# Rebuilding float32 weights from float64 words: an exponent, a product and a float addition replaced by one integer addition

## The chip, the core and the metric

The kernel runs as one program on one core of a Trainium2 chip. The metric is the device time of one execution in microseconds, the median of several executions. Five engines work side by side, each on its own in-order list of instructions: TensorE (PE, matrix products), VectorE (DVE), ScalarE (ACT), GpSimd (POOL) and SyncE (SP, which here only issues transfers). They meet through semaphores.

## The reference

A causal attention with a compressive memory feeds two gated feed-forward layers (B=4, H=8, S=576, D=64; 2304 tokens of 512 channels):

```python
local = softmax(causal(q @ k.T / 8)) @ v
mem   = (phi(q) @ M_prev) / (phi(q) @ z_prev + 1e-6)      # phi(x) = elu(x) + 1
x     = sigmoid(beta) * mem + (1 - sigmoid(beta)) * local
x     = (sigmoid(x @ w_gate) * (x @ w_val)) @ w_out       # width 1536
h     = x @ w_in                                          # width 2048
out   = (h * clip(h + 3, 0, 6) / 6) @ w_out2
```

The five weight matrices of the two layers come to the device as float64. [...]

## The kernel before

**Phase A** runs 32 attention visits (a pair of heads and a range of rows each) and, interleaved with them on PE, six of the twelve hidden blocks of the first layer for the first 1872 tokens. In a visit PE makes scores (`score_part`), DVE takes the row maximum from them (L324), ACT the exponentials (L362), ACT or DVE the normalisation (L390, L392), PE transposes (L402), ACT copies the transposed blocks to SBUF (L404), and PE multiplies with the values (`pv`, L426). POOL makes the products for the memory norm (`prep_phi`, L301 and L305) and writes the memory columns into the rows that are transposed (`memory_rows`, L377). `moe_a` is the interleaved first layer; its gated product on DVE is L488.

**Phase B** does the rest of the first layer: per hidden block the gate and value products (L233 to L235 into tile `g`), a tanh on ACT, the gated product on DVE (L674), its split (L228 on ACT, L229 on DVE, tile `hs`), and the second product into `acc`.

**Phase C** does the second layer by sums of blocks with seven products in place of eight. For each of three groups of tokens `c_load` reads the activations into `xh`, `c_sums` makes three sums on POOL (L735), and `c_block` splits each of seven operands into a tile `xq` (L228, L229; the operand `t4` has one more sum on POOL, L754). The products are L787, those of the second matrix L822. Tile `xt` of the sums and one half of `xh` use the two buffers `wst` in which the float64 weights are staged, so the first group's sums start only when the last weight has been converted.

**Weights** are staged by `w_load` (two matrices' blocks at a time, two buffers `wst`) and converted by `value`: ACT takes the absolute value of the high word (L151), DVE clamps it (L152), cuts and shifts the bits (L153), puts sign and top exponent bit back (L154, in place in the high word), cuts out the exponent (L155), scales the low word by it (L157) and adds it (L158). `convert` and `convert_pair` then split the result into a rounded part (ACT, L163 or L201) and a remainder (DVE, L164 or L202). The work tile `wf` has one buffer. A call handles 1024 elements per partition in phase A (9 calls, "wide") and 512 later (50 calls, "narrow"; 4 of them stand late in phase A, 46 in phase B). The converted weights of phase C go to DRAM and are fetched back in phase C.

The order on PE is written out by hand in phases A and C. On the other engines, and on PE in phase B, a scheduler sets the order when the program is built, by costs of its own; each engine then keeps that order whatever the real durations are.

Of the kernel before, what the change touches and what calls it, by code (L numbers as in the profile page):

```python
# [8 lines left out]
F32 = mybir.dt.float32  # L9
F32R = mybir.dt.float32r  # L10
I32 = mybir.dt.int32
U32 = mybir.dt.uint32
AF = mybir.ActivationFunctionType
ALU = mybir.AluOpType
# [64 lines left out]
class Kernel:  # L79
# [64 lines left out]

    def value(self, st):

        nc = self.nc
        lo, hi = st[:, :, :, 0], st[:, :, :, 1]
        w = self.stage.tile([128, self.wide, 512], F32, name="wf", tag="wf", bufs=1)
        wi, hif, lof = w.bitcast(I32), hi.bitcast(F32), lo.bitcast(F32)  # L150
        nc.scalar.activation(w, hif, AF.Abs)  # L151
        nc.vector.tensor_scalar(w, w, HI_MIN, HI_MAX, op0=ALU.max, op1=ALU.min)  # L152
        nc.vector.tensor_scalar(wi, wi, 0x07FFFFFF, 3, op0=ALU.bitwise_and, op1=ALU.logical_shift_left)  # L153
        nc.vector.scalar_tensor_tensor(hi, hi, -0x40000000, wi, op0=ALU.bitwise_and, op1=ALU.bitwise_or)  # L154
        nc.vector.tensor_scalar(wi, hi, -0x800000, None, op0=ALU.bitwise_and)  # L155
        yield hif
        nc.vector.scalar_tensor_tensor(lof, lo.bitcast(U32), 2.0**-52, w, op0=ALU.mult, op1=ALU.mult)  # L157
        nc.vector.tensor_tensor(hif, hif, lof, op=ALU.add)  # L158

    def convert(self, sl, st):  # L160
        nc = self.nc
        for hif in self.value(st):
            nc.scalar.copy(sl[:, 0], hif)  # L163
        nc.vector.tensor_tensor(sl[:, 1], hif, sl[:, 0].bitcast(F32), op=ALU.subtract)  # L164

    def convert_pair(self, j, up, st):
# [807 lines left out]
```

## Time and profile before

| | |
|---|---|
| median of 3 runs | 1081.23 us (1079.56 to 1082.05) |
| the profiled execution | 1079.94 us, span 1078.2 us |
| busy, share of the span: PE / DVE / ACT / POOL | 96% / 63% / 51% / 8% |
| mean granted TensorE clock | 0.987 |

The span is the time from the first to the last instruction of that execution; what lies around it makes up the rest of its time. Phase A lasts from 0 to about 400 us, phase B to 684 us, phase C to the end. PE counts as busy while a matmul is in flight, so its share says when it had nothing to do, and not how fast it went. PE is waited for or waits; a wait of another engine costs time only if PE comes to wait for it.

### The profile page before, as it was taken

The page shows a single profiled execution, that of the slowest core. Times are in us where ns is not written, and L with a number is a line of the kernel's source. Part 1 is how long each engine was busy: PE and PEld are TensorE (multiplying, and loading weights), DVE is VectorE, ACT ScalarE, POOL GpSimd, SP SyncE. Part 2 cuts the span into 40 slices and gives each one's busy share as a digit, 9 for nine tenths or more (in the row PEclk, how much of TensorE's full clock was granted, in tenths as well). Part 3 has the DMA queues.
Part 4 walks back from the last instruction along what each step waited for, and adds up shares of the span by engine and source line. Part 5 has one row for each costly group of instructions (what it writes and reads, how often), then busy time and mean ns, then how long its engine had stood idle before and what let it go on. Part 6 is the DMA issues. An engine that isn't in the chain of part 4 may idle for free.

```text
span 1078.2 us, 16086 instructions
## 1 busy us (share of the span) xinstructions
PE 1037.6 (96%) x5824; PEld 890.3 (83%) x5824; DVE 684.2 (63%) x1602; ACT 551.5 (51%) x1191; POOL 83.2 (8%) x102
## 2 busy tenths in 40 slices
PE   4789999999999999999999999799999999999998
PEld 2457768877887899999888888688888888888886
DVE  7999885454455348899898988854355333643432
ACT  5989885576556644435434433434344333543432
POOL 3212211110111000000000000320002000000000
PEclk9879999999999999999999999899999999999999
DMA  6645642424242225227586776645305543044511
GB/s 217 220 170 182 202 129 68 141 79 120 59 134 79 64 85 175 93 102 260 216 292 221 257 250 221 228 178 215 122 27 184 186 148 135 1 153 190 215 40 59
DMA packets 66239, 164.87 MB, mean 153 GB/s; under 512 B 8432, under 2 KB 41712, under 8 KB 60272
## 3 DMA queue, kind: packets, MB, share of 16 engines
q1 hardware_dynamic: 66160, 163.85, 44.5%
q8 instruction: 46, 0.75, 0.3%
q14 instruction: 33, 0.27, 0.1%
HBM read 122.76 MB, written 41.06 MB: 152 GB/s over the span
## 4 chain that ended last, share of the span: by engine, by line
PE 85%; DVE 7%; ACT 3%; DMA 2%; issue 1%; POOL 1%; SPq 0%; POOLq 0%; ACTq 0%
PE acc L822 18%; PE pa L787 9%; PE pb L787 7%; PE g L235 6%; PE g L233 6%; PE g L234 6%; PE m L233 5%; PE m L234 5%; PE m L235 5%; PE pv L426 4%; PE t L402 4%; PE s L344 3%; PE acc L233 3%; PE acc L235 3%; PE acc L234 3%; DMA aux<-in_aux 2%
## 5 line engine op out<-in xcount | busy, mean ns | idle before, releaser
L822 PE MATMUL acc<-wslot,hs 128*128 128x512 f32 x864 | 227.8, 395 | 2.2 <-ACT hs L228 2.2
L822 PEld LDWEIGHTS acc<-wslot,hs 128*128 128x128 f32 x864 | 159.5, 188 | 27.7 <-ACT hs L228 3.5
L787 PE MATMUL pa<-xq,wslot 128*128 128x384 f32 x576 | 119.3, 342 | 7.3 <-ACT xq L228 5.4
L787 PEld LDWEIGHTS pa<-xq,wslot 128*128 128x128 f32 x576 | 105.1, 190 | 16.6 <-ACT xq L228 5.8
L235 PE MATMUL g<-xs,wslot 128*128 128x468 f32 (+1 forms) x288 | 106.1, 369 | 0.0
L234 PE MATMUL g<-xs,wslot 128*128 128x468 f32 (+1 forms) x288 | 105.6, 369 | 0.0
L233 PE MATMUL g<-xs,wslot 128*128 128x468 f32 (+1 forms) x288 | 103.9, 369 | 0.0
L362 ACT ACTIVATE P<-P,m 128x192 f32<-128x192 f32 (+4 forms) x144 | 84.1, 586 | 31.2 <-DVE m L324 29.8
L233 PE MATMUL m<-xs,wslot 128*128 128x312 f32 x288 | 93.7, 325 | 0.0
L787 PE MATMUL pb<-xq,wslot 128*128 128x384 f32 x432 | 89.1, 341 | 0.2 <-DVE xq L229 0.2
L234 PE MATMUL m<-xs,wslot 128*128 128x312 f32 x288 | 88.1, 306 | 0.0
L235 PE MATMUL m<-xs,wslot 128*128 128x312 f32 x288 | 87.8, 305 | 0.0
L344 PE MATMUL s<-qk 64*128 64x320 f32 (+3 forms) x320 | 70.8, 502 | 14.3 <-DMA qk<-in_qk 11.8
L787 PEld LDWEIGHTS pb<-xq,wslot 128*128 128x128 f32 x432 | 78.6, 189 | 7.0 <-DVE xq L229 0.7
L851 DVE TENSOR_TENSOR c<-pb,u 128x384 f32<-128x384 f32 x48 | 26.6, 555 | 88.1 <-ACT u L887 87.1
L402 PEld LDWEIGHTS t<-ident,P 128*128 128x128 f32 x464 | 53.8, 145 | 27.2 <-issue 14.5
L799 ACT ACTIVATE r<-c,three 128x384 f32<-128x384 f32 x72 | 44.2, 614 | 61.9 <-DVE c L851 61.9
L402 PE MATMUL t<-ident,P 128*128 128x128 f32 x464 | 68.4, 285 | 7.5 <-POOL P L377 4.1
L229 DVE TENSOR_TENSOR hs<-r,hs 128x384 fp32r<-128x384 f32 x96 | 55.9, 586 | 26.3 <-ACT hs L228 24.8
L404 ACT COPY T<-t 128x512 f32<-128x512 f32 (+2 forms) x128 | 65.7, 540 | 12.1 <-PE t L402 11.9
L324 DVE CUSTOM_DVE_ANT_0 P<-s,mask 128x320 f32<-128x320 f32 (+3 forms) x144 | 62.5, 451 | 14.5 <-PE s L344 14.2
L426 PE MATMUL pv<-T,aux 128*64 128x256 f32 (+2 forms) x512 | 63.4, 377 | 4.5 <-ACT T L404 4.5
(102 smaller groups left out, 1966.9 us busy)
## 6 DMA issues: line engine op xcount, KB each, us to landing
wst<-in_wm SPq DMA_DIRECT2D x68, 512.0 KB, 5.7
wslot<-wd SPq DMA_DIRECT2D x30, 1024.0 KB, 5.0
wd<-wslot SPq DMA_DIRECT2D x16, 1024.0 KB, 4.4
wslot<-wd SPq DMA_DIRECT2D x15, 768.0 KB, 6.3
wd<-wslot SPq DMA_DIRECT2D x8, 768.0 KB, 5.8
qk<-in_qk SPq DMA_DIRECT2D x32, 160.0 KB, 2.3
aux<-in_aux SPq DMA_DIRECT2D x16, 320.0 KB, 3.3
qk<-in_qk SPq DMA_DIRECT2D x16, 288.0 KB, 3.0
```

What stands on the lines that cost most here:

```text
L229: elo.tensor_tensor(lo, src, hi.bitcast(F32), op=ALU.subtract)
L233: nc.tensor.matmul(out, w[0], x[0], start=first, stop=False)
L234: nc.tensor.matmul(out, w[0], x[1], start=False, stop=False)
L235: nc.tensor.matmul(out, w[1], x[0], start=False, stop=last)
L324: self.nc.vector.tensor_tensor_reduce(out=self.row(v, rg, r, 64 + a, 64 + e), in0=ps, in1=mask, scale=-0.125, scalar=3.0e38 if a == 0 else ...
L344: nc.tensor.matmul(ps[:, : e - a], qk[rows, 0, q0 : q0 + 128], qk[rows, 1, a:e], start=True, stop=True)
L362: self.nc.scalar.activation(x, x, AF.Exp, bias=vs["m", rg][:, r : r + 1], scale=-1.0, accum_out=vs["l", rg][:, r : r + 1])
L402: nc.tensor.transpose(ps[:, 128 * n : 128 * n + 128], self.row(v, rg, r, 128 * j, 128 * j + 128), self.ident)
L404: nc.scalar.copy(pr["T", rg][:, 512 * k : 512 * k + c], ps[:, :c])
L426: nc.tensor.matmul(ps[rows, o : o + w], pr["v"][:, j, rows], T[:, c : c + w], start=(n == 0), stop=(n == last), skip_group_check=True,)
L787: nc.tensor.matmul(ps[:, :HC], w[:, i, b, cc], x[:, l, k], start=first and k == 0 and n == 0, stop=last and k == 1 and n == 2, skip_group_ ...
L822: nc.tensor.matmul(a, h[:, i, cc], w[:, l, f], start=first and f == 0 and n == 0, stop=last and f == 1 and n == 2)
```

## The change

The low word is scaled by 2^-29 and rounded to an integer, in place, on POOL (L155 of the new kernel). Sign and top exponent bit are put back into `wf` in place of the high word (L156, was L154). The sum of the two as 32-bit integers is the float32's bit pattern, with the carry into the exponent (L158). The rounded part is now copied from `wf` (L163). L155 and L157 of the old kernel, DVE instructions both, are gone. Line numbers of `value` move: old L151 to L153 are new L152 to L154.

```diff
     def value(self, st):
...
         lo, hi = st[:, :, :, 0], st[:, :, :, 1]
         w = self.stage.tile([128, self.wide, 512], F32, name="wf", tag="wf", bufs=1)
-        wi, hif, lof = w.bitcast(I32), hi.bitcast(F32), lo.bitcast(F32)
+        wi, hif = w.bitcast(I32), hi.bitcast(F32)
         nc.scalar.activation(w, hif, AF.Abs)
         nc.vector.tensor_scalar(w, w, HI_MIN, HI_MAX, op0=ALU.max, op1=ALU.min)
         nc.vector.tensor_scalar(wi, wi, 0x07FFFFFF, 3, op0=ALU.bitwise_and, op1=ALU.logical_shift_left)
-        nc.vector.scalar_tensor_tensor(hi, hi, -0x40000000, wi, op0=ALU.bitwise_and, op1=ALU.bitwise_or)
-        nc.vector.tensor_scalar(wi, hi, -0x800000, None, op0=ALU.bitwise_and)
-        yield hif
-        nc.vector.scalar_tensor_tensor(lof, lo.bitcast(U32), 2.0**-52, w, op0=ALU.mult, op1=ALU.mult)
-        nc.vector.tensor_tensor(hif, hif, lof, op=ALU.add)
+        nc.gpsimd.tensor_scalar(lo, lo.bitcast(U32), 2.0**-29, None, op0=ALU.mult)
+        nc.vector.scalar_tensor_tensor(wi, hi, -0x40000000, wi, op0=ALU.bitwise_and, op1=ALU.bitwise_or)
+        yield w, hif
+        nc.vector.tensor_tensor(hi, wi, lo, op=ALU.add)

     def convert(self, sl, st):
         nc = self.nc
-        for hif in self.value(st):
-            nc.scalar.copy(sl[:, 0], hif)
+        for w, hif in self.value(st):
+            nc.scalar.copy(sl[:, 0], w)
         nc.vector.tensor_tensor(sl[:, 1], hif, sl[:, 0].bitcast(F32), op=ALU.subtract)
```

On DVE at the end of phase B (L674 is the gated product of one hidden block, `xq` an operand of phase C, `c` the first result of phase C), the order before has the last remainder of a weight (L164) behind the last L674:

```order
L674 SCALAR_TENSOR_TENSOR th<-th,g 128x468
L152 TENSOR_SCALAR wf<-wf 128x512
L164 TENSOR_TENSOR wslot<-wst,wslot 128x512
L153 TENSOR_SCALAR wf<-wf 128x512
L229 TENSOR_TENSOR hs<-th,hs 128x468
L154 SCALAR_TENSOR_TENSOR wst<-wst,wf 128x512
L155 TENSOR_SCALAR wf<-wst 128x512
L157 SCALAR_TENSOR_TENSOR wst<-wst,wf 128x512
L158 TENSOR_TENSOR wst<-wst 128x512
L694 SCALAR_TENSOR_TENSOR xp<-acc,xp 128x468 x2
L164 TENSOR_TENSOR wslot<-wst,wslot 128x512
L694 SCALAR_TENSOR_TENSOR xp<-acc,xp 128x468 x2
```

The same engine with the change, from the last conversion on:

```order
L156 SCALAR_TENSOR_TENSOR wf<-wst,wf 128x512
L158 ISA wst<-wst,wf 128x512x2
L164 TENSOR_TENSOR wslot<-wst,wslot 128x512
L674 SCALAR_TENSOR_TENSOR th<-th,g 128x468
L694 SCALAR_TENSOR_TENSOR xp<-acc,xp 128x468 x2
L229 TENSOR_TENSOR hs<-th,hs 128x468
L694 SCALAR_TENSOR_TENSOR xp<-acc,xp 128x468 x2
L674 SCALAR_TENSOR_TENSOR th<-th,g 128x468
L229 TENSOR_TENSOR xq<-xh,xq 128x768 x2
L229 TENSOR_TENSOR hs<-th,hs 128x468
L674 SCALAR_TENSOR_TENSOR th<-th,g 128x468
L229 TENSOR_TENSOR xq<-xt,xq 128x768
```

The last conversion now stands ahead of the last six L674 (three of them are shown), and the operands `xq` of phase C stand among them. The addition is a custom instruction (ISA) over pairs of 16-bit halves, 512x2.

On DVE in phase A, around the first split of activations for the first layer (`xs` from `xc`), the order before has the second conversion's addition:

```order
L385 SCALAR_TENSOR_TENSOR l<-l,a_108 128x5
L306 TENSOR_REDUCE nr<-phw 128x5
L229 TENSOR_TENSOR xs_636<-xc,xs_636 128x312
L324 ISA P,m<-s,mask 128x320
L324 ISA m 128x1
L158 TENSOR_TENSOR wst<-wst 128x1024
```

With the change the third conversion's addition stands there:

```order
L154 TENSOR_SCALAR wf<-wf 128x1024
L229 TENSOR_TENSOR xs_632<-xc,xs_632 128x312
L156 SCALAR_TENSOR_TENSOR wf<-wst,wf 128x1024
L306 TENSOR_REDUCE nr<-phw 128x5
L324 ISA P,m<-s,mask 128x320
L324 ISA m 128x1
L158 ISA wst<-wst,wf 128x1024x2
```

Conversions have moved ahead of the attention: up to the first L488, 5 additions stood on DVE before and 7 stand there now, and on ACT 7 pairs of absolute value and copy in place of 5 ahead of the tanh that belongs to that L488.

On POOL at the start of phase A, the scaling joins the list between the products of a visit (L301, L305) and its memory columns (L377), where before L377 followed L305 at once:

```order
L301 TENSOR_TENSOR phw<-ph,zz 128x64
L305 TENSOR_TENSOR phw<-ph,zz 128x256
L155 TENSOR_SCALAR wst<-wst 128x1024
L377 TENSOR_TENSOR P<-ph,nr 128x5x64
L301 TENSOR_TENSOR phw<-ph,zz 128x64
L305 TENSOR_TENSOR phw<-ph,zz 128x256
L155 TENSOR_SCALAR wst<-wst 128x1024
```

Nine wide scalings stand in phase A; of the 50 narrow ones the last 46 follow each other ahead of the first L735. The order on PE is the same in phases A and C; in phase B some matmuls near the borders of token groups change places.

## Rows read from the trace of the kernel before

**Rows 1.** The page: span, and PE's busy time, share and instructions.

```profile
span 1078.2 us, 16086 instructions
...
PE 1037.6 (96%) x5824; PEld 890.3 (83%) x5824; DVE 684.2 (63%) x1602; ACT 551.5 (51%) x1191; POOL 83.2 (8%) x102
```

**Rows 2.** Busy us by stretch; columns PE, PEld, DVE, ACT, POOL, clock, DMA share, GB/s.

```profile
16.00:66.00 50.00, 37.81 (x200) 21.49 (x200) 49.26 (x136) 46.30 (x112) 11.64 (x14) 0.83 0.57 180
400.00:684.00 284.00, 283.89 (x1401) 258.33 (x1400) 254.56 (x477) 120.92 (x206) 0.00 (x0) 1.00 0.60 211
684.67:692.94 8.27, 2.33 (x6) 1.93 (x7) 7.03 (x6) 3.92 (x6) 8.19 (x4) 0.62 0.58 222
```

**Rows 3.** PE's timeline where phase C begins: start us, us, instruction, idle before it.

```profile
679.09 1.20 PE L787 MATMUL pa<-xq,wslot 128*128 128x384 f32 x6
...
683.51 0.38 PE L235 MATMUL acc<-hs,wslot 128*128 128x468 f32 x1
689.27 0.69 PE L787 MATMUL pa<-xq,wslot 128*128 128x384 f32 x1 [5.38 <-ACT xq L228]
691.30 1.97 PE L787 MATMUL pa<-xq,wslot 128*128 128x384 f32 x5 [1.34 <-DVE xq L229]
...
701.25 1.09 PE L822 MATMUL acc<-wslot,hs 128*128 128x512 f32 x4
```

**Rows 4.** POOL's timeline from 400 to 702 us, the first of its four rows.

```profile
684.67 1.81 POOL L735 TENSOR_TENSOR xt<-xh 128x768 f32<-128x768 f32 x1 [319.82 <-DVE wslot L164]
```

**Rows 5.** DVE's timeline from 640 to 702 us.

```profile
653.80 0.64 DVE L674 SCALAR_TENSOR_TENSOR th<-th,g 128x468 f32<-128x468 f32 x1 [0.59 <-PE g L235]
...
661.45 0.64 DVE L674 SCALAR_TENSOR_TENSOR th<-th,g 128x468 f32<-128x468 f32 x1 [0.46 <-PE g L235]
...
683.76 0.68 DVE L164 TENSOR_TENSOR wslot<-wst,wslot 128x512 fp32r<-128x512 f32 x1
...
686.70 2.07 DVE L800 SCALAR_TENSOR_TENSOR r<-r,c 128x384 f32<-128x384 f32 x1 [0.68 <-ACT r L799]
689.25 2.00 DVE L229 TENSOR_TENSOR xq<-xt,xq 128x768 fp32r<-128x768 f32 x1 [0.48 <-ACT xq L228]
691.33 2.43 DVE L229 TENSOR_TENSOR xq<-xh,xq 128x768 fp32r<-128x768 f32 x1
693.68 0.95 DVE L229 TENSOR_TENSOR xq<-xt,xq 128x768 fp32r<-128x768 f32 x1
```

**Rows 6.** DVE's groups by shape, whole span: busy us, mean ns, idle before.

```profile
L800 DVE SCALAR_TENSOR_TENSOR r<-r,c 128x384 f32<-128x384 f32 x72 | 42.1, 584 | 20.8 <-ACT r L799 20.8
L157 DVE SCALAR_TENSOR_TENSOR wst<-wst,wf 128x512 f32<-128x512 uint32 x50 | 34.6, 692 | 1.2
...
L158 DVE TENSOR_TENSOR wst<-wst 128x512 f32<-128x512 f32 x50 | 34.4, 691 | 6.1 <-ACT wslot L163 3.8
...
L155 DVE TENSOR_SCALAR wf<-wst 128x512 int32<-128x512 int32 x50 | 21.5, 431 | 1.0
...
L158 DVE TENSOR_TENSOR wst<-wst 128x1024 f32<-128x1024 f32 x9 | 11.8, 1315 | 0.1
...
L157 DVE SCALAR_TENSOR_TENSOR wst<-wst,wf 128x1024 f32<-128x1024 uint32 x9 | 11.0, 1225 | 0.0
...
L155 DVE TENSOR_SCALAR wf<-wst 128x1024 int32<-128x1024 int32 x9 | 6.6, 735 | 0.0
```

**Rows 7.** POOL's groups by shape, whole span.

```profile
L735 POOL TENSOR_TENSOR xt<-xh 128x768 f32<-128x768 f32 x3 | 5.6, 1855 | 344.4 <-DVE wslot L164 319.8 <-DMA xh<-x 24.6
L107 POOL MEMSET mask<- 128x576 f32 x1 | 0.6, 583 | 0.0
```

**Rows 8.** ACT's groups by shape: the wide conversions.

```profile
L151 ACT ACTIVATE wf<-wst 128x1024 f32<-128x1024 f32 x9 | 10.5, 1163 | 3.2 <-DMA wst<-in_wm 3.2
L163 ACT CAST wslot<-wst 128x1024 fp32r<-128x1024 f32 x9 | 10.3, 1147 | 1.3 <-DVE wst L154 1.2
```

**Rows 9.** PE's waits from 80 to 160 us, the largest: total us, times, longest.

```profile
PE pv L426 <- ACT T L404: 1.1, 3, 0.8
```

## The prediction

> **What bounds the kernel now.** The page comes first: PE is busy for 1037.6 of 1078.2 us [rows 1], so a shorter DVE list helps only where PE waits for it. The busy times by stretch show where that is [rows 2]. In phase B PE is busy for 283.9 of 284 us at full clock although DVE is at 254.6; nothing can be gained inside it. Two places remain.
>
> The first is the start of phase C, in PE's timeline [rows 3]. The last matmul of phase B starts at 683.51; then PE waits 5.38 and 1.34 us for operands `xq`. [...] At 701.25 the stage runs. From 683.7 to 701.25 there are 36 matmuls L787; at 1.20 us for six they are worth 7.2 us. The hole costs 17.5 - 7.2 = 10.3 us. Its cause stands on POOL: the first sum L735 starts at 684.67, released by L164 [rows 4], the last remainder of a weight, at 683.76 on DVE [rows 5]. The sums need the staging buffers.
>
> The second is the start of phase A. From 16 to 66 us PE is busy for 37.8 of 50 us at a mean clock of 0.83, DVE for 49.3 and ACT for 46.3 [rows 2]. Both are full; PE follows them. After that PE hardly waits: the largest entry from 80 to 160 us sums to 1.1 us [rows 9].
>
> **The change part by part.** *Two DVE instructions go.* A narrow call loses L155 and L157, 0.431 + 0.692 = 1.12 us; a wide call 0.735 + 1.225 = 1.96 us [rows 6].
>
> *The addition becomes another instruction.* The float addition took 0.69 us for 512 and 1.32 for 1024 elements [rows 6]. The new one moves the same bytes as 1024 and 2048 halves. If halves go in pairs it stays at 0.69, if one by one it takes what 1024 elements take, 1.32, and a wide one about 2.6. I take 0.80 and 1.45, near the low end since the bytes are the same: +0.11 and +0.14 a call. [...] No run here shows such an instruction yet.
>
> *POOL gets the scaling.* No row has it. The lowest bound is the memset, 0.583 us for 576 elements [rows 7], so 0.52 for 512; the highest is the two-operand L735, 1.855 us for 768, so 1.24. I take 0.9 (1.8 wide), midway, since it reads one operand and writes one. [...]
>
> *POOL slows DVE.* While the four sums ran, 8.19 us of POOL [rows 2], three DVE instructions that read two SBUF tensors took 2.07, 2.00 and 2.43 us [rows 5], where they take 0.58 [rows 6] and 0.95 [rows 5] alone. That is 1.49 + 1.05 + 1.48 = 4.0 us lost, 0.49 us per us of POOL. I charge that rate to each scaling.
>
> *ACT's copy* from `wf` in place of the strided high word, the earlier release of `lo`, and the order of phase B's matmuls I cost at nothing: ACT is at 121 of 284 us in phase B [rows 2], and in phase A its instructions remain as many and as large. Without that cover the copies would be worth a few us either way.
>
> *Sum for phase B's DVE*, 46 calls: -46 x 1.12 = -51.7; addition +5.1; contention 46 x 0.9 x 0.49 = +20.3; net -26 us. With the low bounds it is -51.7 + 11.7 = -40, with the high ones -51.7 + 29.0 + 28.0 = +5. The cover against a delay is DVE's idle time there, 284 - 254.6 = 29 us [rows 2].
>
> *The hole.* In the built order the last L164 now stands ahead of the last six L674, which come 7.65 us apart [rows 5]: five spacings, 38 us before PE leaves phase B. The contention is not in that order, so DVE may run late by up to 20 us; the last conversion still ends near 660 or 665. The sums (8.2 us of POOL) and the splits of `xq` then fit before 684. The hole closes: **-10 us** (0 to -11). What is late next is the first gated products of phase C, some tenths.
>
> *The start.* Here the order works the other way: 7 conversions in place of 5 stand ahead of the first L488. On DVE five calls become shorter by 1.96 - 0.14 = 1.82 us, so -9.1; two more calls cost 2 x 0.735 (as L155) + 2 x 1.225 (as L157) + 1.45 = 5.4 each, so +10.8; seven scalings cost 7 x 1.8 x 0.49 = +6.2. Together +7.9. On ACT two more pairs of L151 and L163 stand ahead, 2 x (1.163 + 1.147) = +4.6 us [rows 8], against 3.7 us idle. On POOL the scaling precedes L377 and on SP two staging loads move ahead of attention loads; both press the same way. The two delays overlap, some of DVE's falls on instructions nobody waits for, and PE's later wait of 1.1 us may go: **+5 us**. Low bound -2 (only ACT's excess of 0.9, less the later wait and some DVE time); high bound: the addition at 2.6 (five calls save 0.7 each, two cost 6.5: +9.6) and POOL at 2.5 (+8.6), so +18.
>
> *Total:* 1079.94 (the profiled execution's own time) - 10 + 5 = **1075 us**. That execution lies 1.3 us below the median of 1081.23, inside the runs' spread of 2.5 us; I leave the number there. A measurement of this kernel can tell about 0.2%, 2.2 us, from no change, so "same" is 1079.1 to 1083.4.
>
> **The rivals.** *Slower: POOL eats the saving.* Place: DVE in phase B. Each further us of a narrow scaling costs DVE 0.49 us a call. From 1.6 us on (0.7 more than I took) 46 x 0.35 = 16 of the 26 us are gone, the last conversion is again at phase B's end, and the hole stays. The start is dearer too: seven wide scalings at 3.2 us cost 11 us in place of 6.2, so some +9, together 1089; at the high bound of the start 1098. For it: no row has a conversion of integers on POOL, and the sums hit DVE hard [rows 5]. Against it: one operand is read, not two. Chance 0.11.
>
> *Slower: halves one by one.* At 1.32 us the addition costs 46 x 0.52 = 24 us more, so the hole stays as well; at the start two dear calls and five hardly cheaper ones make DVE's +7.9 into some +15, of which I put +10 on the path: 1090. For it: 1024 halves are 1024 elements. Against it: the bytes of [rows 6]. [...] Chance 0.06.
>
> *The start costs nothing.* If the two earlier conversions fill only waits, the time is 1079.9 - 10 - 2 = 1068. For it: in phase A POOL ran only 11.6 of 50 us [rows 2], and the whole list of phase A loses 9 x 1.96 = 17.6 us of DVE. Against it: the idle time left is 0.7 us on DVE. Chance 0.14.
>
> *The start takes the hole's gain back.* With +10 at the start (DVE's +7.9 wholly on the path, and PE longer at the lower clock, 0.83 now) it is 1080, no change. For it: DVE's 98% there. Against it: some of the two delays is the same delay. Chance 0.11.
>
> That the edit does not do what it says would show in the built order; both instructions are gone there, so only durations are open.
>
> **How the numbers follow.** Forecast (hole closed, start +1 to +8: 1071 to 1078) 0.58, rivals 0.11, 0.06, 0.14, 0.11. The likeliest is 1075. The range takes the forecast, the start for nothing down to 1065, no change, and the slower rivals up to 1088; left out are their upper half (0.09) and a larger gain (0.03). Faster: 0.58 + 0.14 and a little of the last (0.01) = 0.73; same: most of the last, 0.08; slower: 0.11 + 0.06 and the rest of the last (0.02) = 0.19.
>
> **What would show it.** Right: L735's wait for L164 ends well before 684, PE has no hole there and the clock stays 1.0; the scaling takes near 0.9 us, the addition near 0.8; PE's first matmul of the first layer comes some 5 us later. Wrong: L735 still starts behind phase B; DVE instructions with two SBUF operands stay near 0.69 beside the scaling; PE waits on L674's or L229's results in phase B; or the first layer starts earlier than before.

## The result, and the profile after

The changed kernel takes 1095.24 us (median of 4 runs, 1094.48 to 1100.27) against 1081.64 for the kernel before, a ratio of 1.0138 over all runs with the 95% interval [1.0105, 1.0172] (the two medians alone give 1.0126): slower by 13.6 us. The forecast was 1075 with a range up to 1088. The hole at the start of phase C closed as forecast; two other places lost more than it gave.

The page of the changed kernel; span, and busy time of the engines, against [rows 1]:

```profile
span 1093.4 us, 16109 instructions
...
PE 1042.1 (95%) x5824; PEld 893.6 (82%) x5824; DVE 649.8 (59%) x1484; ACT 547.9 (50%) x1191; POOL 193.3 (18%) x161
```

DVE works 34 us less than before and POOL 110 us more, as the change intends. To see where the time went, PE's groups by line are read for when the same work starts (min/median/max ns, then first and last start in us). `m` and `ha` belong to the first layer in phase A; `hs` and `acc` to phase B. L233, L234 and L235 are the three matmuls of which each large product is made, since weights and activations are split into a rounded part and a remainder. First the kernel before, then the changed one:

```profile
L233 PE MATMUL m<-xs,wslot x288: 301/305/415, 66.2 to 402.4; 128*128 128x312 f32 x144
L233 PE MATMUL m<-ha,wslot x144: 299/305/417, 117.8 to 417.8; 128*128 128x312 f32 x144
L233 PE MATMUL acc<-hs,wslot x144: 352/372/379, 425.1 to 681.8; 128*128 128x468 f32 x96, 128*128 128x432 f32 x48
L235 PE MATMUL acc<-hs,wslot x144: 353/372/379, 426.5 to 683.5; 128*128 128x468 f32 x96, 128*128 128x432 f32 x48
```

```profile
L233 PE MATMUL m<-xs,wslot x288: 301/305/627, 69.4 to 415.9; 128*128 128x312 f32 x144
L233 PE MATMUL m<-ha,wslot x144: 299/305/417, 127.9 to 430.6; 128*128 128x312 f32 x144
L233 PE MATMUL acc<-hs,wslot x144: 352/372/378, 437.3 to 705.7; 128*128 128x468 f32 x96, 128*128 128x432 f32 x48
L235 PE MATMUL acc<-hs,wslot x144: 353/372/381, 438.8 to 707.3; 128*128 128x468 f32 x96, 128*128 128x432 f32 x48
```

Two marks are used from here on. The **start** is the first L233 `m<-ha`: 117.8 us before, 127.9 after, 10.1 later; of this, 3.1 us are there at the first L233 `m<-xs`, the first matmul of the first layer (66.2 and 69.4). (The lag at the first `g` of phase B, 404.6 against 418.1, is 13.5, so another 3.4 us go in the rest of phase A.) **Phase B** is the time from the first `acc` of L233 to the last of L235: 683.5 - 425.1 = 258.4 us before, 707.3 - 437.3 = 270.0 after. At the first L822 the lag has shrunk from 23.8 us (683.5 to 707.3) to 14.3 (701.2 to 715.5): the hole gave 9.5 back.

That the hole closed stands in POOL's timeline of the changed kernel, where the first sum L735 starts 37 us before phase B ends instead of behind it [rows 4], and in PE's timeline, where phase C follows on phase B with six matmuls L787 in 1.21 us [rows 3]:

```profile
670.13 1.85 POOL L735 TENSOR_TENSOR xt<-xh 128x768 f32<-128x768 f32 x1 [17.58 <-DMA xh<-x]
```

```profile
707.35 0.38 PE L235 MATMUL acc<-hs,wslot 128*128 128x468 f32 x1
707.57 1.21 PE L787 MATMUL pa<-xq,wslot 128*128 128x384 f32 x6
```

What PE waits for ahead of the start is in its waits from 25 to 80 us (total, times, longest); before, the entry for L377 was 4.1 us:

```profile
PE t L402 <- POOL P L377: 10.4, 3, 4.8
PE s L344 <- ACT th L486: 4.5, 1, 4.5
```

POOL's timeline of the changed kernel shows why the memory rows L377 are late: they stand behind wide scalings L155, and start as these end. All three waits for them lie ahead of the first `m<-xs`.

```profile
40.47 3.44 POOL L155 TENSOR_SCALAR wst<-wst 128x1024 int32<-128x1024 uint32 x1 [2.41 <-DMA wst<-in_wm]
43.99 0.88 POOL L377 TENSOR_TENSOR P<-ph,nr 128x320 f32<-128x320 f32 x1
...
52.71 3.76 POOL L155 TENSOR_SCALAR wst<-wst 128x1024 int32<-128x1024 uint32 x1 [6.36 <-DVE m L324]
56.55 0.95 POOL L377 TENSOR_TENSOR P<-ph,nr 128x256 f32<-128x256 f32 x1
```

The other 7.0 us of the start are lost behind the first `m<-xs`, from 74.5 to 86.4 us. PE waits for the tanh L486 of the first layer on ACT (the scores `s` use the same buffers as `m`) and then for a row maximum L324 (before, it waited 2.1 us for L324 there and not for L486); after the first wait the granted clock is 0.50, and the matmuls `m<-xs` start 0.26 us apart (84.18, 84.44, 84.70 us), where it was 0.15 ahead of the wait (73.89, 74.04, 74.19). First PE's timeline, then ACT's, then the busy times from 79.15 to 86.4 us (columns as in [rows 2]):

```profile
79.15 1.22 PE L344 MATMUL s<-qk 64*128 64x256 f32 x2 [4.52 <-ACT th L486]
82.60 1.22 PE L344 MATMUL s<-qk 64*128 64x256 f32 x2 [2.24 <-DVE m L324]
```

```profile
77.72 1.05 ACT L163 CAST wslot<-wf 128x1024 fp32r<-128x1024 f32 x1
78.67 0.43 ACT L486 ACTIVATE th<-m 128x312 f32<-128x312 f32 x1
```

```profile
79.15:86.40 7.25, 5.01 (x15) 3.33 (x15) 6.18 (x16) 3.84 (x8) 3.63 (x2) 0.50 0.58 215
```

The tanh is 7.2 us later than before (71.49 us). Ahead of it on ACT stand the two conversions more of which the prediction speaks, L152 and L163 of each; in the 4.5 us of PE's wait ACT runs other attention work and one such L163.

In phase B, where before PE waited for nothing, it now waits for the splits of the activations (PE's waits from 425 to 710 us):

```profile
PE g L234 <- DVE xs L229: 3.7, 3, 2.1
PE acc L234 <- DVE hs L229: 2.7, 1, 2.7
PE g L233 <- ACT xs L228: 0.8, 2, 0.5
```

The waits for `xs` come at three of the four chunk changes. The one for `hs` comes at 677.6 us, where DVE splits `xq` for phase C beside POOL's sums, in 2.24 us each where the next `xq` from `xh` behind the sums takes 0.96 (681.09 us), and the split `hs` stands behind (DVE's timeline). A closed hole does not need this: in x2, x7 and x10 below the hole is closed and PE waits for no `hs`.

```profile
670.86 4.48 DVE L229 TENSOR_TENSOR xq<-xh,xq 128x768 fp32r<-128x768 f32 x2 [2.31 <-ACT xq L228]
675.26 2.24 DVE L229 TENSOR_TENSOR hs<-th,hs 128x468 fp32r<-128x468 f32 x1
```

And the busy times by stretch (columns as in [rows 2]). In phase B DVE is far from full. The last two rows are one of the waits and what follows it: 2.4 us lost, then 10 us at a clock of 0.83, in which PE is busy but slower: its matmuls `g<-xs` start 0.39 us apart from 560.54 to 563.66 us and 0.21 from 563.95 on.

```profile
418.00:707.00 289.00, 281.87 (x1368) 254.31 (x1367) 236.09 (x388) 120.30 (x208) 85.03 (x50) 0.99 0.58 213
550.00:560.00 10.00, 7.59 (x36) 6.06 (x34) 7.61 (x11) 4.31 (x9) 6.38 (x4) 1.00 0.49 199
560.00:570.00 10.00, 10.00 (x40) 8.72 (x41) 9.86 (x20) 5.06 (x10) 0.00 (x0) 0.83 0.50 179
```

The new instructions themselves, by shape (busy us, mean ns, idle before); L155 is POOL's scaling of the low 32-bit word of each float64 weight, L158 the integer addition:

```profile
L156 DVE SCALAR_TENSOR_TENSOR wf<-wst,wf 128x512 int32<-128x512 int32 x50 | 38.7, 775 | 1.2
L158 DVE CUSTOM_DVE_ANT_0 wst<-wst,wf 128x1024 uint16<-128x1024 uint16 x50 | 36.7, 733 | 4.4
L154 DVE TENSOR_SCALAR wf<-wf 128x512 int32<-128x512 int32 x50 | 28.1, 562 | 1.1
...
L158 DVE CUSTOM_DVE_ANT_0 wst<-wst,wf 128x2048 uint16<-128x2048 uint16 x9 | 11.0, 1221 | 0.1
```

```profile
L155 POOL TENSOR_SCALAR wst<-wst 128x512 int32<-128x512 uint32 x50 | 83.0, 1659 | 199.6 <-DMA wst<-in_wm 129.5 <-DVE ha L229 41.1 <-DVE wf L153 12.2
L155 POOL TENSOR_SCALAR wst<-wst 128x1024 int32<-128x1024 uint32 x9 | 30.1, 3350 | 28.3 <-DMA wst<-in_wm 21.9 <-DVE m L324 6.4
```

The addition costs a little less than was assumed (0.73 and 1.22 us; 0.80 and 1.45 assumed). The scaling costs 1.66 and 3.35 us where 0.9 and 1.8 were assumed, about 3.2 ns per element and well above the prediction's upper bound of 1.24 us for a narrow one.

### The profile page after: what moved, and what is told of

The parts are those of the page before. It is cut to its first block, busy times and chain, and to the rows that moved or that the text cites. A ratio compares the mean times of both kernels' runs of the same rounds, so it can differ in the third digit from the quotient of the medians.

```text
span 1093.4 us, 16109 instructions
## 1 busy us (share of the span) xinstructions
PE 1042.1 (95%) x5824; PEld 893.6 (82%) x5824; DVE 649.8 (59%) x1484; ACT 547.9 (50%) x1191; POOL 193.3 (18%) x161
## 4 chain that ended last, share of the span: by engine, by line
PE 60%; DVE 21%; DMA 9%; ACT 5%; issue 4%; SPq 1%; POOL 0%; DVEq 0%; ACTq 0%
PE acc L822 17%; PE pa L787 9%; PE pb L787 6%; DMA wst<-in_wm 5%; PE m L233 5%; PE m L234 4%; PE m L235 4%; PE pv L426 4%; PE t L402 4%; DVE wf L156 3%; PE s L344 3%; DVE wst L158 3%; DVE wf L154 2%; DVE wf L153 2%; DVE wslot L164 2%
## 5 line engine op out<-in xcount | busy, mean ns | idle before, releaser
L822 PE MATMUL acc<-wslot,hs 128*128 128x512 f32 x864 | 227.9, 395 | 2.9 <-ACT hs L228 2.2
L822 PEld LDWEIGHTS acc<-wslot,hs 128*128 128x128 f32 x864 | 159.5, 188 | 28.7 <-ACT hs L228 3.5
L155 POOL TENSOR_SCALAR wst<-wst 128x512 int32<-128x512 uint32 (+1 forms) x59 | 113.1, 1917 | 227.9 <-DMA wst<-in_wm 151.4
L787 PE MATMUL pa<-xq,wslot 128*128 128x384 f32 x576 | 117.3, 338 | 1.1 <-ACT u L887 0.6
L787 PEld LDWEIGHTS pa<-xq,wslot 128*128 128x128 f32 x576 | 103.7, 188 | 9.9 <-ACT u L887 0.9
L234 PE MATMUL g<-xs,wslot 128*128 128x468 f32 (+1 forms) x288 | 107.0, 372 | 3.7 <-DVE xs L229 3.7
L235 PE MATMUL g<-xs,wslot 128*128 128x468 f32 (+1 forms) x288 | 107.0, 372 | 0.0
L233 PE MATMUL g<-xs,wslot 128*128 128x468 f32 (+1 forms) x288 | 105.7, 372 | 0.8 <-ACT xs L228 0.8
L362 ACT ACTIVATE P<-P,m 128x192 f32<-128x192 f32 (+4 forms) x144 | 83.8, 584 | 37.7 <-DVE m L324 36.7
L233 PE MATMUL m<-xs,wslot 128*128 128x312 f32 x288 | 94.3, 327 | 0.3 <-ACT th L486 0.3
L344 PE MATMUL s<-qk 64*128 64x320 f32 (+3 forms) x320 | 72.2, 504 | 18.3 <-DMA qk<-in_qk 10.1
L234 PE MATMUL m<-xs,wslot 128*128 128x312 f32 x288 | 88.6, 308 | 0.0
L235 PE MATMUL m<-xs,wslot 128*128 128x312 f32 x288 | 88.3, 307 | 0.0
L787 PE MATMUL pb<-xq,wslot 128*128 128x384 f32 x432 | 87.8, 338 | 0.0
L787 PEld LDWEIGHTS pb<-xq,wslot 128*128 128x128 f32 x432 | 77.9, 188 | 6.3
L402 PE MATMUL t<-ident,P 128*128 128x128 f32 x464 | 70.3, 292 | 12.2 <-POOL P L377 10.4
L152 ACT ACTIVATE wf<-wst 128x512 f32<-128x512 f32 (+1 forms) x59 | 43.9, 745 | 64.1 <-DVE wst L158 37.4
L229 DVE TENSOR_TENSOR hs<-r,hs 128x384 fp32r<-128x384 f32 x96 | 56.4, 592 | 26.8 <-ACT hs L228 25.4
L324 DVE CUSTOM_DVE_ANT_0 P<-s,mask 128x320 f32<-128x320 f32 (+3 forms) x144 | 62.6, 452 | 16.1 <-PE s L344 15.8
```

What stands on the lines that cost most here:

```text
L155: nc.gpsimd.tensor_scalar(lo, lo.bitcast(U32), 2.0**-29, None, op0=ALU.mult)
L229: elo.tensor_tensor(lo, src, hi.bitcast(F32), op=ALU.subtract)
L233: nc.tensor.matmul(out, w[0], x[0], start=first, stop=False)
L234: nc.tensor.matmul(out, w[0], x[1], start=False, stop=False)
L235: nc.tensor.matmul(out, w[1], x[0], start=False, stop=last)
L324: self.nc.vector.tensor_tensor_reduce(out=self.row(v, rg, r, 64 + a, 64 + e), in0=ps, in1=mask, scale=-0.125, scalar=3.0e38 if a == 0 else ...
```

## The experiments

All numbers of the runs in one table. "Conv." counts the additions of conversions that run on DVE ahead of the first L488; "m<-xs" is the first L233 `m<-xs`; "L377" and "L486" are PE's waits for L377 on POOL (25 to 80 us) and for the tanh L486 where it frees a score buffer; "profiled" is the time of the execution from which the columns to its left come; the ratio is to runs of the kernel before on the same chip. One execution can lie off the median: x1's profiled one took 5.6 us more, x3's 3.1 more, x5's 2.7 less.

| run | conv. | m<-xs | start | phase B | L377 | L486 | profiled | median | ratio, interval |
|---|---|---|---|---|---|---|---|---|---|
| before | 5 | 66.2 | 117.8 | 258.4 | 4.1 | 0 | 1079.9 | 1081.64 | 1 |
| changed | 7 | 69.4 | 127.9 | 270.0 | 10.4 | 4.5 | 1095.1 | 1095.24 | 1.0138 [1.0105, 1.0172] |
| x1_scale_dve | 7 | 78.7 | 129.7 | 258.8 | 6.5 | 0 | 1087.6 | 1082.01 | 1.0031 [1.0014, 1.0047] |
| x2_scale_act | 6 | 67.9 | 120.9 | 259.6 | 4.5 | 0 | 1077.7 | 1075.63 | 0.9959 [0.9944, 0.9974] |
| x3_l377_dve | 6 | 69.8 | 122.2 | 270.6 | 0 (0.7 on DVE) | 0 | 1086.0 | 1082.84 | 1.0029 [1.0016, 1.0041] |
| x4_old_plus_pool | 5 | 72.6 | 130.3 | 259.0 | 8.0 | 2.9 | 1100.4 | 1098.47 | 1.0169 [1.0145, 1.0192] |
| x5_new_in_a | 7 | 71.9 | 130.7 | 258.4 | 11.4 | 3.8 | 1090.9 | 1093.52 | 1.0116 [1.0094, 1.0137] |
| x6_new_in_b | 5 | 65.9 | 117.3 | 270.8 | 4.4 | 0 | 1085.2 | 1087.12 | 1.0057 [1.0039, 1.0076] |
| x7_old_a_act_b | 5 | 63.2 | 117.4 | 259.6 | 3.2 | 0 | 1071.2 | 1071.89 | 0.9920 [0.9899, 0.9941] |
| x8_b_program_order | 7 | 69.6 | 126.7 | 324.4 | 11.3 | 4.3 | 1147.7 | 1147.79 | 1.0626 [1.0592, 1.0661] |
| x9_rows_first | 6 | 74.0 | 122.4 | 272.2 | 6.7 | 0 | 1088.7 | 1089.11 | 1.0091 [1.0067, 1.0114] |
| x10_xs_before_second | 7 | 70.9 | 128.5 | 260.5 | 10.2 | 4.4 | 1087.1 | 1085.65 | 1.0047 [1.0028, 1.0066] |
| x11_xs_before_both | 7 | 70.9 | 128.9 | 271.2 | 10.0 | 4.4 | 1093.7 | 1093.28 | 1.0118 [1.0099, 1.0137] |
| x12_both_orders | 6 | 74.1 | 122.5 | 269.5 | 6.2 | 0 | 1086.8 | 1086.51 | 1.0057 [1.0041, 1.0073] |
| x13_orders_that_worked | 6 | 72.1 | 122.1 | 263.0 | 7.9 | 0 | 1079.0 | 1079.18 | 0.9987 [0.9976, 0.9998] |
| x14_act_b_order_of_change | 6 | 69.1 | 121.2 | 260.1 | 4.6 | 0 | 1078.0 | 1077.84 | 0.9960 [0.9945, 0.9975] |

**Which engine scales.** Three runs move one instruction each, a fourth puts POOL's scaling into the kernel before.

```
x1:  nc.gpsimd.tensor_scalar(lo, ...)  ->  nc.vector.tensor_scalar(lo, ...)          # L155
x2:  nc.gpsimd.tensor_scalar(lo, ...)  ->  nc.scalar.activation(lo, lo.bitcast(U32), AF.Copy, scale=2.0**-29)
x3:  self.nc.gpsimd.tensor_tensor(out, ph, nr, ...)  ->  self.nc.vector.tensor_tensor(...)   # L377
x4, in the kernel before:
+ nc.gpsimd.tensor_scalar(lof, lo.bitcast(U32), 2.0**-29, None, op0=ALU.mult)
- nc.vector.scalar_tensor_tensor(lof, lo.bitcast(U32), 2.0**-52, w, op0=ALU.mult, op1=ALU.mult)
+ nc.vector.scalar_tensor_tensor(lof, lof, 2.0**-23, w, op0=ALU.mult, op1=ALU.mult)
```

Expected of x1:

> The changed kernel with one edit: L155, the scaling of the low word, runs on DVE in place of POOL; the integer addition stays. Two theories of the late start (the first L233 m<-ha at 117.8 us before, 127.9 after) are weighed. POOL theory: POOL's 3.35 us scalings stand ahead of the memory rows L377 in POOL's order, and PE's transposes L402 wait for those. Then the 10 us that PE waits for L377 in 25 to 80 us fall to about 4, DVE takes some 1.2 us more for each of 6 wide conversions, and the first L233 m<-ha comes at 119 to 123 us. Order theory: the late start comes from conversions that stand earlier in DVE's and ACT's orders (7 ahead of the first L488 after, 5 before, 6 here). Then it comes at 125 us or later, since DVE has more to do, not less. In phase B (first acc to last acc of L235, 258.4 us before, 270.0 after) DVE takes about 50 x 0.7 = 35 us more and loses its wait for POOL: if POOL's part in the conversion is what stretches the phase, it comes to 258 to 262 us; if DVE's order alone does, it stays at 266 us or more. Whole kernel: 1080 to 1088 us by the POOL theory, 1092 to 1102 by the order theory.

The whole and phase B came as the POOL theory had them, 1082.0 and 258.8 us although DVE has one instruction more per conversion. The start did not: 129.7, as the order theory had it. In this run's trace 7 conversions stand ahead of the first L488, not 6, and POOL has no scaling at all; PE still waits 6.5 us for L377, whose operands come from DVE. The start is that of an execution 5.6 us slower than the median that gives the 1082.0, so how late it is in the others is not shown.

> The changed kernel with L155 on ACT (a copy with a factor) in place of POOL; the integer addition stays. POOL then has what it had before the change, and 5 conversions stand ahead of the first L488 as before. Both theories of the start expect the first L233 m<-ha at 118 to 122 us (ACT takes some 1.1 us more for each of 5 conversions), with at most 4 us of PE waiting for L377. What this run tells apart is phase B: if POOL's scaling stretches it (its latency in the chain of a conversion, or DVE instructions made longer by POOL at the same time), first acc to last acc is back at 258 to 262 us, and L154 (562 and 855 ns after, its like 422 and 698 before) and L156 (775 after, 690 before) are back at the times of before; if it is the order of DVE's list, it stays at 266 or more. Whole kernel 1070 to 1078 us by the first, 1080 to 1086 by the second.

With the scaling on ACT the kernel is faster than before the change, 1075.6 us. Phase B is back at 259.6, the start at 120.9, and DVE's instructions are back at the times of before: L154 at 426 and L156 at 690 ns in the groups of DVE. So without POOL's scaling all three are gone in this run. For the start that is no proof of POOL's part: 6 conversions stand ahead of the first L488 here, not 5, against 7 in the changed kernel, and x1 was late without it.

> The changed kernel, POOL scaling kept, with the memory rows L377 moved from POOL to DVE. POOL theory: the transposes no longer wait for anything behind a scaling in POOL's order; L377 costs DVE some 0.5 us each; the first L233 m<-ha comes at 117 to 121 us in place of 127.9, and the whole kernel gains 6 to 10 us on the changed one (1085 to 1089). Against it: if the wait only passes to the next late thing (POOL's phi L304 and L305 behind a scaling, or the maxima that DVE does later), it comes at 124 us or later and the kernel stays within 4 us of 1095. Phase B has no L377: 266 to 272 us by every theory.

The start comes 5.7 us earlier and the kernel gains 12.4, more than expected (9.2 in the profiled execution). It is not the whole start, and 6 conversions stand ahead of the first L488 here, one fewer than in the changed kernel. In place of L377 PE waits for what DVE and ACT prepare, as PE's waits from 25 to 80 us show:

```profile
PE t L402 <- ACT phw L298: 6.0, 1, 6.0
PE t L402 <- ACT P L390: 5.4, 2, 5.2
```

> The kernel before with one instruction more per conversion: POOL scales the low word by 2^-29 in place (as in the change), and the old product takes the scaled word. DVE's and ACT's instructions are those of before in number and size, and 5 conversions stand ahead of the first L488 as before, so POOL's part is seen by itself. POOL theory: PE waits some 10 us for L377 in the start, the first L233 m<-ha comes at 124 to 130 us, DVE's two-input and in-place instructions get 5 to 25% longer, and phase B gets 8 us or more longer than before: 1095 to 1110 us in all. Order theory: the POOL instruction lies beside other work; 1079 to 1086 us, the first L233 m<-ha at 117 to 121.

POOL alone, with the old arithmetic (here it writes float32) and 5 conversions ahead of the first L488 as before, makes the start as late (130.3) as the whole change does. That excludes the two conversions placed earlier, on which the prediction built, as a necessary cause; x1 does the same for POOL's scaling, as far as its one execution shows. But phase B stays at 259.0, against the POOL theory's 8 us: POOL's work and DVE's longer instructions are there and do no harm. The hole at the start of phase C remains (PE waits 7.8 us for `xq`).

**Which phase.** The two arithmetics are chosen by the width of the call: wide in phase A, narrow in phase B.

```
x5:  value, convert = new if self.wide == 2 else old
x6:  value, convert = new if self.wide == 1 else old
x7:  as x6, with L155 as nc.scalar.activation(lo, lo.bitcast(U32), AF.Copy, scale=2.0**-29)
```

> The new arithmetic with POOL's scaling in phase A only (the wide conversions), the old arithmetic in phase B. If the two losses are separate, this one has the late start of the changed kernel (first L233 m<-ha at 126 to 130 us) and a phase B as before the change (first to last acc 257 to 261 us); the hole at the start of phase C, which closes where DVE is early, is open again in part (5 to 8 us of PE waiting for xq, as before the change and with the old arithmetic and POOL: 5.4 and 7.8 us). Whole kernel 1090 to 1098 us. If the start is not POOL's doing in the wide conversions but the order that the scheduler finds for the whole program, the start moves by 5 us or more.

> The reverse: the old arithmetic in phase A, the new one with POOL's scaling in phase B. DVE's order in phase B is then that of the changed kernel, instruction for instruction. First L233 m<-ha at 116 to 121 us as before; phase B 267 to 272 us as in the changed kernel (270.0) and with L377 on DVE (270.6), since its instructions and their order are the same; the hole stays closed. Whole kernel 1081 to 1087. If phase B comes back at 259 to 262, its stretch came from what phase A hands over (the time at which transfers are started), and the kernel takes 1070 to 1075.

> The old arithmetic in phase A, and in phase B the new one with the low word scaled on ACT. It joins the better half of each: the start of before (first L233 m<-ha at 116 to 121 us), a phase B of 258 to 261 us as with ACT scaling throughout (259.6), no hole at the start of phase C (less than 1 us of PE waiting for xq). 1068 to 1074 us, faster than before the change by 7 to 12; with ACT scaling throughout it was 1075.6. If ACT's load in phase A was not what cost 3 us there, it stays at 1074 to 1077.

All three came in or at the edge of the expected ranges. The losses are separate: x5 has the late start and no long phase B (its hole is open, as before the change), x6 the long phase B alone, and x6's DVE list in phase B is that of the changed kernel. x7 has neither and is the best version found, 1071.9 us, faster than before by 0.8%. PE's waits from 425 to 710 us show phase B without a wait and phase C without a hole:

```profile
PE pa L787 <- ACT u L887: 0.6, 1, 0.6
PE pa L787 <- ACT u L877: 0.5, 1, 0.5
```

**Which order.** What stayed open was why POOL's scaling stretches phase B with the new arithmetic (270) and not with the old (259). The scheduler gives the two different DVE lists. The next runs keep every instruction on its engine and move only its place, x8 by the program's order in all of phase B, the others by ordering edges between two instructions of one engine. The scheduler then builds its lists anew around the edges, and more moves than the pairs named. The lists in the traces show it, against the changed kernel: in x9 12 instructions of POOL, some 90 of DVE and 45 of ACT stand elsewhere in phase A; in x10 some 70 of DVE, 25 of ACT and 80 of PE in phase B, and about as many in x14. So these runs compare whole lists, not single places. (x13 has the lists of x9 in phase A and of x10 in phase B.)

```
x8:   with tc.manual_schedule(engines={mybir.EngineType.DVE}): k.phase_b()
x9:   self.tc.add_manual_dep(scaling[k], rows[k], order only)      # L155 behind L377, k = 0 to 6
x10:  self.tc.add_manual_dep(masked[k], split, order only)         # L156 of conversions 32, 40, 48, 56 behind the last xs L229 of chunks 1 to 4
x11:  self.tc.add_manual_dep(clipped[k], split, order only)        # L153 of conversions 31, 39, 47, 55, the same
x12:  x9 and x11;   x13:  x9 and x10
x14:  x2, with the four xs behind L158 of conversions 32, 40, 48, 56
```

> The changed kernel with POOL's scaling in place, and DVE's order in phase B as the program is written instead of as the scheduler puts it (same instructions, only DVE's list in phase B is moved). In the changed kernel 11.6 us are lost in phase B where splits xs and hs stand in DVE's list behind a conversion that waits for its transfer. Order theory: with the splits ahead of the conversions of the same step, PE's waits for xs and hs (7.2 us) go, and phase B takes 258 to 264 us; 1083 to 1090 in all. POOL theory (its latency stretches each conversion): phase B stays at 267 to 275 whatever the order. A third way: in program order a conversion waits behind the gate L674, which waits for PE, and weights come late: then PE waits for wslot, which the waits show.

Something like the third way came, and far dearer than either theory: 324 us. PE's waits from 425 to 765 us name the gate that DVE's list reaches late; the third way had weights late instead.

```profile
PE g L233 <- DVE th L674: 39.5, 9, 14.7
```

The run does not decide between the theories, but shows that the same instructions in another DVE list cost 54 us.

> The changed kernel with one order changed: in phase A each of the first seven wide scalings L155 stands directly behind the memory rows L377 of its step in POOL's list instead of directly ahead; POOL keeps every instruction, and PE's list is the same. If it is the place of L377 behind the 3.35 us scalings that makes the start late, PE's waits for L377 (10.4 us) fall to 5 or less as with L377 on DVE, and the first L233 m<-ha comes at 118 to 123 us in place of 127.9: 1083 to 1090 us in all. If it is POOL's load on DVE (longer DVE instructions) or the scaling's lateness for the conversion, the start stays at 125 to 129 us and the kernel at 1092 to 1097.

The start is at 122.4, 5.5 us earlier, but not by the way expected. PE's wait for L377 fell less than expected, to 6.7 us, and the first `m<-xs`, behind these waits, is 4.6 us later than in the changed kernel:

```profile
L233 PE MATMUL m<-xs,wslot x288: 301/305/415, 74.0 to 407.2; 128*128 128x312 f32 x144
```

The gain comes behind it: PE waits neither for L486 nor, next to it, 2.2 us for L324, and the longest L233 `m<-xs` takes 415 ns, where it is 627 in the changed kernel. The list has 6 conversions ahead of the first L488 in place of 7, so the run does not separate POOL's order from the conversions' places. POOL's timeline of this run shows what is left: L377 stands ahead of the scaling and waits for DVE.

```profile
36.48 0.72 POOL L377 TENSOR_TENSOR P<-ph,nr 128x320 f32<-128x320 f32 x1 [6.09 <-DVE l L385]
37.29 3.38 POOL L155 TENSOR_SCALAR wst<-wst 128x1024 int32<-128x1024 uint32 x1
```

> The changed kernel with DVE's list changed at the four later chunks of phase B: the four splits xs stand ahead of L156 and L158 of the second conversion of the pair, about as they do in the list of the kernel with ACT scaling (phase B 259.6 us), where the changed kernel has them behind both conversions. POOL's scaling stays. Order theory: PE's waits for xs (3.7 us) go to under 1.5, and with them the lowered clock behind them; phase B 260 to 266 us, the whole 1085 to 1091. POOL theory (the scaling's 1.66 us in each conversion's chain, and the longer DVE instructions): phase B stays at 267 to 272.

Phase B falls to 260.5 with POOL's scaling untouched, and no wait for `xs` is left: the order theory. The wait for `hs`, which the edges don't name, is gone too; the splits `xq` from `xh`, two of which ran ahead of that `hs` in the changed kernel, take 1.25 us each in the mean of the five up to 700 us, for 1.49 in the changed kernel up to 710 us. DVE's timelines at the second chunk show the two orders, first that of the changed kernel, where both conversions are through before the first split, then that of x10. From the second L153 to the first `xs` it is 510.66 - 507.50 = 3.2 us in the one, 511.51 - 510.25 = 1.3 in the other; in the changed kernel PE waits 1.26 us for this split.

```profile
507.50 0.43 DVE L153 TENSOR_SCALAR wf<-wf 128x512 f32<-128x512 f32 x1 [0.73 <-ACT wf L152]
507.96 0.86 DVE L154 TENSOR_SCALAR wf<-wf 128x512 int32<-128x512 int32 x1
508.86 0.69 DVE L156 SCALAR_TENSOR_TENSOR wf<-wst,wf 128x512 int32<-128x512 int32 x1
509.69 1.05 DVE L158 CUSTOM_DVE_ANT_0 wst<-wst,wf 128x1024 uint16<-128x1024 uint16 x1
510.66 1.19 DVE L229 TENSOR_TENSOR xs<-x,xs 128x468 fp32r<-128x468 f32 x2
```

```profile
510.25 0.43 DVE L153 TENSOR_SCALAR wf<-wf 128x512 f32<-128x512 f32 x1 [0.73 <-ACT wf L152]
510.71 0.88 DVE L154 TENSOR_SCALAR wf<-wf 128x512 int32<-128x512 int32 x1
511.51 1.19 DVE L229 TENSOR_TENSOR xs<-x,xs 128x468 fp32r<-128x468 f32 x2
```

> As the run before, but the splits xs stand ahead of the whole pair, so that nothing in DVE's list that waits for a staged transfer or for POOL is ahead of them. Order theory: no PE wait for xs at all, phase B 258 to 264 us, the whole 1082 to 1089. POOL theory: 267 us or more, since conversions stay as long as they were; conversions that are late by these 3 to 5 us would show as PE waiting for wslot, which no run with the scheduler's own list has shown.

A miss by both theories' letter: the waits for `xs` are gone as the order theory had it, but phase B is at 271.2, and the lateness has moved to `hs`, which nobody had named (PE's waits from 425 to 710 us):

```profile
PE acc L234 <- DVE hs L229: 5.3, 3, 2.6
```

> The changed kernel with both orders: memory rows ahead of the scalings on POOL in phase A, and the splits xs ahead of the pair on DVE in phase B. Every instruction of the change is there, on the engine where the change has it. If the two orders are what the change costs, their gains add: 1095 less 8 (5 to 10) less 8 (4 to 11) = 1079 us, 1074 to 1086, about the kernel before the change; what is left against 1071.9 (old arithmetic in A, ACT scaling in B) is POOL's load on DVE in the start. If the losses are POOL's load, 1092 to 1097.

The start is that of x9 (122.5), phase B as in x11 (269.5) and not as expected; the kernel at 1086.5 is past the range by half a microsecond.

> The changed kernel with the order of x9 on POOL (rows ahead of scalings) and that of x10 on DVE (splits xs ahead of L156 and L158 of the second conversion). If the two losses are separate, the start is that of x9 (first L233 m<-ha 122.4 us) and phase B that of x10 (260.5): 1095.2 less 6.1 less 9.6 = 1079.5 us, 1076 to 1083, the time of the kernel before. If they hang together (the earlier start moves the transfers under phase B and the lists no longer fit), phase B is at 266 to 272 again and the kernel at 1085 to 1091.

1079.18, at 1079.5 expected: with every instruction of the change on its engine and nothing but two sets of ordering edges added, the 13.6 us are gone. Phase B is 2.5 us longer than in x10 (PE waits 1.8 us for `xs`).

> The kernel with ACT scaling throughout (1075.6 us, phase B 259.6), its DVE list tied at the four later chunks of phase B so that the splits xs stand behind both conversions of the pair, as in the changed kernel; POOL has no scaling. If the order alone costs, PE waits for xs come back (3 us or more in sum) and phase B takes 264 to 271, the whole 1080 to 1087. If the order costs only where POOL stretches the conversions (L158 and L154 longer by a tenth to a third with POOL), phase B stays at 259 to 262 and the whole at 1074 to 1078.

Phase B is 260.1 and PE waits 0.4 us for `xs`: with POOL free of the scaling, the changed kernel's order at these splits does next to no harm (33, 41, 49 and 57 additions of conversions ahead of the four `xs` in both; in x10 one fewer each). The same timeline of x14 shows the difference: both conversions stand ahead of the first split here too, and from the second L153 to that split it is 503.29 - 501.03 = 2.3 us in place of 3.2.

```profile
501.03 0.43 DVE L153 TENSOR_SCALAR wf<-wf 128x512 f32<-128x512 f32 x1 [0.73 <-ACT wf L152]
501.49 0.43 DVE L154 TENSOR_SCALAR wf<-wf 128x512 int32<-128x512 int32 x1
501.95 0.69 DVE L156 SCALAR_TENSOR_TENSOR wf<-wst,wf 128x512 int32<-128x512 int32 x1
502.68 0.69 DVE L158 CUSTOM_DVE_ANT_0 wst<-wst,wf 128x1024 uint16<-128x1024 uint16 x1
503.29 1.19 DVE L229 TENSOR_TENSOR xs<-x,xs 128x468 fp32r<-128x468 f32 x2
```

So the waits for `xs` need both: conversions that POOL makes longer, and a list that has the splits behind them. Taking either away brings phase B back by 9 to 10 us. Since the rest of the list moved as well in both runs, the part of `hs` in this is not separated.

## Why the prediction was wrong

**The hole, -10 us: right.** It gave 9.5 us, and by the forecast step: the last conversion left DVE well before phase B's end, and the sums started at 670.13. The rival "POOL eats the saving" had the hole stay from a scaling of 1.6 us on; the scaling is at 1.66 and the hole closed, since DVE's loss to POOL was smaller than the rate charged. In a narrow call the DVE instructions that differ took 436 + 422 + 690 + 431 + 692 + 691 = 3362 ns before, 475 + 562 + 775 + 733 = 2545 after and 423 + 424 + 689 + 690 = 2226 with the scaling off POOL (x1, without its own L155). POOL costs the call's own DVE instructions 0.32 us for 1.66 us of its work, 0.19 per us, not 0.49. The call gained 0.82 us where 0.57 were forecast.

**The addition: right.** 0.69 us alone (x1) and 0.73 beside POOL; the rival of halves one by one falls.

**The start, +5 us: half of the 10.1 that were measured, and the cause is in part open.** The term that was mis-sized is the wide scaling, 1.8 us assumed and 3.35 measured; the step left without a price is "On POOL the scaling precedes L377 [...]; both press the same way". PE waits 10.4 us for L377 in place of 4.1, but only 3.1 us of lag are left of that at the first `m<-xs`, since PE waited for other things there before: its waits from 25 to 66 us sum to 10.2 us before and 13.2 after. The other 7.0 us come behind it: 4.5 for the tanh L486, 2.2 for L324, and 2.5, an estimate, by a clock of 0.50 in 5.01 us of matmuls (half of them), less 2.1 that PE waited for L324 at the same place before. That is the prediction's own step on ACT, two more conversions ahead of this tanh: their L152 and L163 of 1.1 us each are 4.4 us, with the lag 7.5 (an estimate), and the tanh is 7.2 us later. The prediction set 3.7 us of ACT's idle time against this step, let the delays overlap and gave nothing to the clock.

Which of the two makes the start late is not settled. Without x4, the start goes with the conversions ahead of the first L488: 117.3 to 117.8 us with 5, 120.9 to 122.5 with 6, 126.7 to 130.7 with 7. x4 is late (130.3) with 5 and POOL's scaling, x1 (129.7, in an execution 5.6 us above its median) with 7 and no scaling on POOL. The runs that brought the start back with POOL's scaling kept, x3, x9, x12 and x13, all have 6; no run moves L377 with the conversions left in place.

**Phase B, 0 us: wrong.** The step that failed is "The cover against a delay is DVE's idle time there", 29 us. The sum over the phase was right (DVE is less busy than before), but idle time summed over 284 us covers nothing at the four chunk changes, where PE needs `xs` at once and DVE's list has two conversions ahead of the splits. x14 keeps that order there and takes the scaling off POOL, x10 keeps POOL's scaling and changes the order, and in both the 10 us are gone. The prediction did name this as a sign of being wrong ("PE waits on L674's or L229's results in phase B") without pricing it. Of the 11.6 us, 4.5 are PE's waits for `xs`, 2.7 the wait for `hs`, and another 1.7, an estimate (10 x 0.17), the 10 us at a clock of 0.83 (it was 1.0 in all of phase B before). 1.3 us are no loss but the mark: PE's new list has the first `acc` earlier. From the first `g` to the last `acc` it is 278.9 us before, 279.0 in x1, x2 and x7, and 289.2 in the changed kernel, 10.3 more. The remaining 1.4 us were not assigned.

**The sum by the right sizes,** from profiled execution to profiled execution: 1079.9 + 12.2 (the lag at the first `acc`, 425.1 to 437.3) + 11.6 (phase B) - 9.5 (hole) + 0.9 (phase C, first to last L822: 372.9 and 373.8) = 1095.1, with 1095.1 measured. The rival "POOL eats the saving" had "slower" at the right size (1089 to 1098); its scaling of over 1.6 us and its dearer start came, but the hole that it kept open closed, and the loss in phase B was not in it.

## What to carry to other kernels

An instruction put on an idle engine is not free: here L377, behind scalings of 3.44 and 3.76 us in POOL's list, started 0.08 us after each had ended. So look up who is next in that list and who waits for that one, and price the new instruction by a like one on the same data types (float32 rows had put the narrow scaling at 1.24 us at most, and it took 1.66). A wait that grows is not yet the time lost: compare when the bound engine reaches the same instruction in both kernels, ahead of the wait and behind it. And before a run counts as the exchange of two instructions, compare the whole lists: the scheduler may have moved a hundred others. A sum of idle time over a phase is no cover for a list in which an urgent instruction stands behind deferrable ones; look at the few places where the bound engine needs something new. Where such work must be placed, try the engine that has room in that phase: the old arithmetic in phase A and ACT's scaling in phase B beat both kernels (1071.9 us).

## What the runs showed of the hardware

POOL's conversion of uint32 words, 8 bytes apart, to scaled int32 took 1659 ns for 512 and 3350 for 1024 elements per partition, 3.2 and 3.3 ns each; the same instruction took 425 and 700 ns on DVE (x1) and 678 and 1179 on ACT (x2). On POOL it takes 2.4 to 4.8 times as long.

DVE instructions got longer beside POOL's scaling, by different amounts. The narrow L154 with one input took 562 ns for 424 with the scaling off POOL (x1), a third more; L153 with one input 475 for 423, L156 with two 775 for 689, L158 with two 733 for 690, L164 with two 704 for 689. In the old arithmetic beside POOL (x4) the mask with one input took 530 for 422, the sign's instruction with two 739 for 690. The prediction took its rate from instructions with two inputs. Whether the inputs make the difference was not tested: L158 needs its own call's scaling to be done, and so runs less beside POOL than L154 does, 12.1 of its 36.7 us beside a scaling, of L154's 28.1 us 17.8 (timelines of DVE and POOL, changed kernel).
